# Re-tiling a 32-head attention and an MLP on one Trainium2 core: head quads outermost, scores in row strips, the second product in column strips, a quarter of the exponentials on VectorE, every queue's order planned ahead

## Chip, core and metric

The kernel runs on one core of one Trainium2 chip. The metric is device time in microseconds (us), the median of several runs; lower is better. The engines in what follows are TensorE (PE; its weight loads are PEld), VectorE (DVE), ScalarE (ACT), GpSimd (POOL) and SyncE (SP, which here only issues DMAs). PSUM has eight banks, each 128 partitions by 512 f32; SBUF is the large on-chip memory.

## What is computed

An attention branch `a` and an MLP branch `b` on the same input, mixed by a per-row gate `g`. S = 2048 rows, D = 640, H = 32 heads of Dh = 20, F = 1536; all inputs are bf16.

```python
g = sigmoid((x * gate_w).sum(-1, keepdims=True))
q, k, v = split_heads(x @ wqkv)                    # 32 heads of 20
p = softmax(einsum("bhqd,bhkd->bhqk", q, k) * 20**-0.5)
a = merge_heads(einsum("bhqk,bhkd->bhqd", p, v)) @ wo
h = x @ w1 + b1
b = (h * tanh(softplus(h))) @ w2                   # mish
out = g * a + (1 - g) * b
```

The softmax needs 32 x 2048 x 2048 exponentials: as tiles of 128 keys by 1,024 (two heads by 512 queries) that is 1,024 tiles.

## The kernel before

**Tiling.** The outer loop runs over four chunks of 512 query rows (`qc`); inside it, 16 groups of two heads (`emit_group`, L387); inside that, 16 key tiles `j` of 128 keys. One such step is called a slot here; there are 4 x 16 x 16 = 1,024.

**A slot.** Two matmuls (L395) make scores, keys on the partitions and 512 queries along the row, for two heads; each contracts over only 20 rows and sits in its own 32-row strip of the PE array (`tile_position`). They write `Sp`, two PSUM banks. One ACT instruction (L406) takes exp of the whole 128 x 1024 tile into `E` (bf16, two buffers). Then eight pairs of weight load and matmul (L412) use each 128 x 128 block of `E` as weights and stream the 21 columns of `VA` (20 values and a column of ones, which sums the denominators) into `acc`. After 16 slots DVE takes the reciprocal of the denominators (L421) and scales into `O_qc` (L423).

**Filler work.** Everything else waits in queues of small units, and `pump_slot` (L351) emits units after each slot as long as a credit (460 per slot in the first chunk, 340 later) pays for their cost: K projections (`kt_units`, L143, cast at L150), V projections (`v_units`, L186, cast L193), Q projections (`qt_unit`, L208, cast L215), the MLP's first product and mish (`mlp_ht_unit`: L223, then an exp on ACT at L231, four DVE passes and a DVE reciprocal at L241), its second product (`mlp_b_units`, L261), and for the chunk before, transposes of the attention output (L288) and the output projection (L304, L318) with the gate mix (L311 to L329). What is left at a chunk's end is emitted in one go (`drain_all`, L378).

**Start and end.** x is brought in transposed by one DMA transpose (L88) and, per chunk, a smaller one (L439). The first K and V projections (L143, L171) wait for it. The last chunk's output projection comes after all exponentials. A Tile scheduler keeps the order in which the code emits; each engine runs its own queue in that order and waits on semaphores.

**PSUM.** `Sp` has two buffers of two banks, `acc` two, the filler units two banks in all.

Of the kernel before, what the change touches and what calls it, by code (L numbers as in the profile page):

```python
# [8 lines left out]
P = 128  # L10
ACT = mybir.ActivationFunctionType
ALU = mybir.AluOpType
F32 = mybir.dt.float32
BF16 = mybir.dt.bfloat16


@with_exitstack
def kernel(
# [12 lines left out]
    nc = tc.nc  # L31

    _, S, D = A_x.shape
    F = B_w1.shape[1]
    H = 32
    DH = D // H
    KT = D // P
    FT = F // P
    NS = S // P
    QC = 512  # L40
    NQC = S // QC
    NU = QC // P
    NPAIR = H // 4
    NG = H // 2
    ROWB = 32
    inv_sqrt_dh = float(DH) ** -0.5
    CB = 512
    CH = CB // 2

    x2d = A_x[0]  # L50
    out2d = out[0]

    consts = ctx.enter_context(tc.tile_pool(name="consts", bufs=1))
    wqp = consts.tile([P, KT, NPAIR, P], BF16, tag="wqp")
    ident = consts.tile([P, P], BF16, tag="ident")
    wo_sb = consts.tile([P, KT, D], BF16, tag="wo_sb")
    w1_sb = consts.tile([P, KT, F], BF16, tag="w1_sb")
    w2_sb = consts.tile([P, FT, D], BF16, tag="w2_sb")
    b1bf = consts.tile([P, FT], BF16, tag="b1bf")
    b1f = consts.tile([P, FT], F32, tag="b1f")  # L60
    g_t = consts.tile([P, NS], F32, tag="g_t")
    kT_all = consts.tile([P, NPAIR, S], BF16, tag="kT_all")
    VA = consts.tile([P, NS, H, DH + 1], BF16, tag="VA")

    aps = ctx.enter_context(tc.tile_pool(name="aps", bufs=2, space=bass.MemoryType.PSUM))
    xtc_pool = ctx.enter_context(tc.tile_pool(name="xtc", bufs=2))
    qtc_pool = ctx.enter_context(tc.tile_pool(name="qtc", bufs=3))
    e_pool = ctx.enter_context(tc.tile_pool(name="e_pool", bufs=2))
    opool = ctx.enter_context(tc.tile_pool(name="opool", bufs=1))
    otpool = ctx.enter_context(tc.tile_pool(name="otpool", bufs=1))  # L70
    actpool = ctx.enter_context(tc.tile_pool(name="actpool", bufs=1))
    mishp = ctx.enter_context(tc.tile_pool(name="mishp", bufs=2))
    bpool = ctx.enter_context(tc.tile_pool(name="bpool", bufs=2))
    smallp = ctx.enter_context(tc.tile_pool(name="smallp", bufs=2))
    dpool = ctx.enter_context(tc.tile_pool(name="dpool", bufs=1))
    outp = ctx.enter_context(tc.tile_pool(name="outp", bufs=2))

    xt_ctx = ExitStack()
    xt_ctx.__enter__()
    xtpool = xt_ctx.enter_context(tc.tile_pool(name="xtpool", bufs=1))  # L80
    xT = xtpool.tile([P, KT, S], BF16, tag="xT")

    stage_ctx = ExitStack()
    stage_ctx.__enter__()
    stpool = stage_ctx.enter_context(tc.tile_pool(name="stpool", bufs=1))
    Wq = stpool.tile([P, KT, D], BF16, tag="Wq")
    nc.scalar.dma_start(Wq, A_wqkv[:, 0:D].rearrange("(kt p) c -> p kt c", p=P))
    nc.sync.dma_start_transpose(  # L88
        out=xT[:, :, :], in_=x2d.rearrange("s (kt p) -> s kt p", p=P)
    )  # L90
    wv0 = xtpool.tile([P, KT, 4 * DH], BF16, tag="wvp", bufs=2)
    nc.scalar.dma_start(
        out=wv0[:, :, :],
        in_=A_wqkv[:, 2 * D : 2 * D + 4 * DH].rearrange("(kt p) c -> p kt c", p=P),
    )
    gw = xtpool.tile([P, KT, 1], BF16, tag="gw")
    nc.scalar.dma_start(gw, gate_w.rearrange("(kt p o) -> p kt o", p=P, o=1))
    wk0 = xtpool.tile([P, KT, P], BF16, tag="wkp", bufs=2)
    nc.gpsimd.memset(wk0, 0.0)
    for r in range(4):  # L100
        col0 = 64 * (r // 2) + ROWB * (r % 2)
        nc.scalar.dma_start(
            out=wk0[:, :, col0 : col0 + DH],
            in_=A_wqkv[:, D + r * DH : D + (r + 1) * DH].rearrange(
                "(kt p) c -> p kt c", p=P
            ),
        )
    nc.sync.dma_start(b1bf, B_b1.rearrange("(ft p) -> p ft", p=P))
    nc.gpsimd.dma_start(wo_sb, A_wo.rearrange("(kt p) c -> p kt c", p=P))
    nc.gpsimd.dma_start(w1_sb, B_w1.rearrange("(kt p) c -> p kt c", p=P))  # L110
    nc.gpsimd.dma_start(w2_sb, B_w2.rearrange("(ft p) c -> p ft c", p=P))

    nc.gpsimd.memset(wqp, 0.0)
    for h in range(H):
        p, r = divmod(h, 4)
        col0 = 64 * (r // 2) + ROWB * (r % 2)
        nc.gpsimd.tensor_copy(
            out=wqp[:, :, p, col0 : col0 + DH],
            in_=Wq[:, :, h * DH : (h + 1) * DH],
        )  # L120
    stage_ctx.__exit__(None, None, None)
    make_identity(nc, ident)
    nc.vector.tensor_copy(b1f, b1bf)
    nc.gpsimd.memset(VA, 1.0)

    def kt_units(p, wk=None):
        if wk is None:
            wk = xtpool.tile([P, KT, P], BF16, tag="wkp", bufs=2)
            nc.gpsimd.memset(wk, 0.0)
            for r in range(4):  # L130
                h = 4 * p + r
                col0 = 64 * (r // 2) + ROWB * (r % 2)
                nc.sync.dma_start(
                    out=wk[:, :, col0 : col0 + DH],
                    in_=A_wqkv[:, D + h * DH : D + (h + 1) * DH].rearrange(
                        "(kt p) c -> p kt c", p=P
                    ),
                )

        def chunk(sc):  # L140
            pk = aps.tile([P, CB], F32, tag="t")
            for kt in range(KT):
                nc.tensor.matmul(  # L143
                    pk[:, 0:QC],
                    lhsT=wk[:, kt, 0:P],
                    rhs=xT[:, kt, sc * QC : (sc + 1) * QC],
                    start=(kt == 0),
                    stop=(kt == KT - 1),
                )
            nc.vector.tensor_copy(  # L150
                out=kT_all[:, p, sc * QC : (sc + 1) * QC], in_=pk[:, 0:QC]
            )

        return [(1200, (lambda sc=sc: chunk(sc))) for sc in range(NQC)]

    def v_units(p, wv=None):
        if wv is None:
            wv = xtpool.tile([P, KT, 4 * DH], BF16, tag="wvp", bufs=2)
            nc.sync.dma_start(
                out=wv[:, :, :],  # L160
                in_=A_wqkv[:, 2 * D + 4 * p * DH : 2 * D + 4 * (p + 1) * DH].rearrange(
                    "(kt p) c -> p kt c", p=P
                ),
            )

        def unit(st):
            pv = aps.tile([P, CB], F32, tag="t")
            for kt in range(KT):
                lhsT = xT[:, kt, st * P : (st + 1) * P]
                if p == 0:  # L170
                    nc.tensor.matmul(  # L171
                        pv[:, 0 : 4 * DH],
                        lhsT=lhsT,
                        rhs=wv[:, kt, :],
                        start=(kt == 0),
                        stop=False,
                    )
                    nc.tensor.matmul(
                        pv[:, 4 * DH : 4 * DH + 1],
                        lhsT=lhsT,  # L180
                        rhs=gw[:, kt, 0:1],
                        start=False,
                        stop=(kt == KT - 1),
                    )
                else:
                    nc.tensor.matmul(  # L186
                        pv[:, 0 : 4 * DH],
                        lhsT=lhsT,
                        rhs=wv[:, kt, :],
                        start=(kt == 0),  # L190
                        stop=(kt == KT - 1),
                    )
            nc.vector.tensor_copy(  # L193
                out=VA[:, st, 4 * p : 4 * p + 4, 0:DH],
                in_=pv[:, 0 : 4 * DH].rearrange("p (h d) -> p h d", d=DH),
            )
            if p == 0:
                nc.scalar.activation(
                    g_t[:, st : st + 1], pv[:, 4 * DH : 4 * DH + 1], ACT.Sigmoid
                )  # L200

        return [(260, (lambda st=st: unit(st))) for st in range(NS)]

    def qt_unit(p, xTc, qTc_p):
        def unit():
            pq = aps.tile([P, CB], F32, tag="t")
            for kt in range(KT):
                nc.tensor.matmul(  # L208
                    pq[:, 0:QC],
                    lhsT=wqp[:, kt, p, 0:P],  # L210
                    rhs=xTc[:, kt, 0:QC],
                    start=(kt == 0),
                    stop=(kt == KT - 1),
                )
# [312 lines left out]
```

## Time and profile before

Three runs took 1384.87, 1405.74 and 1419.17 us; the median is 1405.74 us. The profiled execution's span, from the first to the last instruction, is 1383.0 us, so it belongs with the fastest of the three.

| | busy us | share of the span | instructions |
|---|---|---|---|
| PE (matmuls) | 1235.3 | 89% | 12384 |
| PEld (weight loads) | 589.6 | 43% | 12384 |
| ACT | 1053.3 | 76% | 1138 |
| DVE | 463.9 | 34% | 1093 |
| POOL | 28.6 | 2% | 51 |

The profile also gives the TensorE clock that was granted, as a share of full speed: its mean is 0.608. Matmuls are pipelined and their ends are modelled, so a matmul's listed duration holds some latency, and the distance between starts is the better measure of what one costs. The DMA engines moved 16.91 MB, 12 GB/s over the span. The first exponential starts at 64.3 us.

### The profile page before, as it was taken

What the parts mean: (1) busy time and instruction counts of PE and PEld (TensorE: products, weight loads), DVE (VectorE), ACT (ScalarE), POOL (GpSimd) and SP (SyncE); (2) the same over time, 40 slices, a digit from 0 to 9 for tenths busy, and PEclk for the clock granted to TensorE, in tenths of its full rate; (3) what the DMA queues carried; (4) which work ended last, traced back from release to release, by engine and by line L of the source; (5) the groups of instructions that cost most, each with busy time, mean ns of one, the idle gap of its engine ahead of it and who ended that gap; (6) DMA issues with size and microseconds to landing.
All of it is one profiled execution on the core that took longest, in us unless ns stands there. A gap on an engine that the chain in (4) does not pass through costs nothing.

```text
span 1383.0 us, 28359 instructions
## 1 busy us (share of the span) xinstructions
PE 1235.3 (89%) x12384; PEld 589.6 (43%) x12384; DVE 463.9 (34%) x1093; ACT 1053.3 (76%) x1138; POOL 28.6 (2%) x51
## 2 busy tenths in 40 slices
PE   0699999988999988998889998998889988998887
PEld 0354444544444444443434444443434444453333
DVE  0222222377722576410101477410001476510002
ACT  0286666987768877698998777698998787699995
POOL 7000000000000000000000000000000000000000
PEclk9975555975585555795555555695555555695555
DMA  9600000000000000000000000000000000000000
GB/s 185 109 8 7 8 7 7 2 1 1 13 8 11 11 1 1 1 21 1 1 1 11 11 1 1 1 2 1 1 2 6 16 2 1 1 2 1 1 1 20
DMA packets 53086, 16.91 MB, mean 12 GB/s; under 512 B 49408, under 2 KB 52096, under 8 KB 52960
## 3 DMA queue, kind: packets, MB, share of 16 engines
q1 hardware_dynamic: 47456, 9.30, 4.6%
q0 software_dynamic: 912, 4.75, 1.2%
q10 hardware_dynamic: 4592, 1.03, 0.6%
q8 instruction: 97, 1.59, 0.5%
q14 instruction: 29, 0.24, 0.1%
HBM read 7.21 MB, written 2.62 MB: 7 GB/s over the span
## 4 chain that ended last, share of the span: by engine, by line
PE 67%; ACT 25%; issue 3%; DMA 3%; DVE 1%; ACTq 0%
PE Sp L395 26%; ACT E L406 25%; PE acc L412 15%; PE ph L223 8%; PE pk L143 5%; PE pb L261 4%; DMA xT<-in_A_x_dram 3%; PE pq L208 3%; PE pa L304 3%; PE pv L186 3%; PE pt L288 1%; ACTq L406 0%; PE pv L171 0%; ACT e_sb L231 0%; DVE d L311 0%
## 5 line engine op out<-in xcount | busy, mean ns | idle before, releaser
L406 ACT ACTIVATE E<-Sp 128x1024 bf16<-128x1024 f32 x1024 | 1006.0, 1022 | 223.6 <-PE Sp L395 213.0
L395 PE MATMUL Sp<-qTc_p,kT_all 20*128 20x512 bf16 x2048 | 589.2, 559 | 0.0
L412 PEld LDWEIGHTS <-E 128*128 128x128 bf16 x8192 | 335.7, 106 | 471.1 <-ACT E L406 376.9
L412 PE MATMUL acc<-VA,E 128*128 128x21 bf16 x8192 | 398.1, 182 | 95.5 <-ACT E L406 93.5
L241 DVE RECIPROCAL rd<-rd 128x256 f32<-128x256 f32 x96 | 167.4, 1744 | 0.8
L395 PEld LDWEIGHTS <-kT_all 20*128 20x128 bf16 x2048 | 104.3, 98 | 51.5 <-issue 18.2
L223 PE MATMUL ph<-xTc,w_sb 128*128 128x256 bf16 x480 | 119.0, 403 | 0.1
L421 DVE RECIPROCAL rden<-acc 128x8 f32<-128x8 f32 x64 | 12.4, 193 | 297.4 <-PE acc L412 297.4
L223 PEld LDWEIGHTS <-w_sb 128*128 128x128 bf16 x480 | 51.7, 128 | 57.4 <-issue 42.6
L234 DVE SCALAR_TENSOR_TENSOR e_sb<-e_sb 128x256 f32<-128x256 f32 x96 | 40.4, 421 | 100.5 <-ACT e_sb L231 99.6
L215 DVE CAST qTc_p<-pq 128x512 bf16<-128x512 f32 x32 | 22.1, 691 | 148.8 <-PE Sp L395 98.6
L231 ACT ACTIVATE e_sb<-ph,b1f 128x256 f32<-128x256 f32 x96 | 45.4, 473 | 33.8 <-PE ph L223 29.9
L143 PE MATMUL pk<-xT,wk 128*128 128x512 bf16 x140 | 66.0, 548 | 0.0
L208 PE MATMUL pq<-xTc,wqp 128*128 128x512 bf16 x160 | 64.5, 492 | 0.0
L261 PE MATMUL pb<-w_sb,actT 128*128 128x512 bf16 x192 | 58.0, 419 | 0.1
L150 DVE CAST kT_all<-pk 128x512 bf16<-128x512 f32 x32 | 22.1, 691 | 96.3 <-PE pk L143 96.3
L186 PE MATMUL pv<-wv,xT 128*128 128x80 bf16 x560 | 50.7, 237 | 0.0
L193 DVE CAST VA<-pv 128x80 bf16<-128x80 f32 x128 | 30.4, 243 | 57.7 <-PE pv L186 51.5
L143 PE MATMUL pk<-xT,wk_118 128*128 128x512 bf16 x20 | 7.2, 544 | 44.4 <-DMA xT<-in_A_x_dram 44.4
L243 DVE SCALAR_TENSOR_TENSOR actT<-ph,b1f,rd 128x256 bf16<-128x256 f32 x96 | 45.8, 478 | 0.1
L186 PEld LDWEIGHTS <-xT 128*128 128x128 bf16 x560 | 33.4, 117 | 23.2 <-issue 23.0
L261 PEld LDWEIGHTS <-actT 128*128 128x128 bf16 x384 | 28.5, 101 | 33.3 <-issue 24.1
(101 smaller groups left out, 351.9 us busy)
## 6 DMA issues: line engine op xcount, KB each, us to landing
w_sb<-in_B_w_dram POOLq DMA_DIRECT2D x2, 1920.0 KB, 31.1
out_dram<-ot SPq DMA_DIRECT2D x16, 160.0 KB, 1.8
Wq<-in_A_wqkv_dram ACTq DMA_DIRECT2D x1, 800.0 KB, 4.9
wo_sb<-in_A_wo_dram POOLq DMA_DIRECT2D x1, 800.0 KB, 24.5
wv<-in_A_wqkv_dram SPq DMA_DIRECT2D x7, 100.0 KB, 2.3
wk<-in_A_wqkv_dram SPq DMA_DIRECT2D x28, 25.0 KB, 2.6
wv_114<-in_A_wqkv_dram ACTq DMA_DIRECT2D x1, 100.0 KB, 10.7
wk_118<-in_A_wqkv_dram ACTq DMA_DIRECT2D x4, 25.0 KB, 29.7
```

What stands on the lines that cost most here:

```text
L143: nc.tensor.matmul(pk[:, 0:QC], lhsT=wk[:, kt, 0:P], rhs=xT[:, kt, sc * QC : (sc + 1) * QC], start=(kt == 0), stop=(kt == KT - 1),)
L186: nc.tensor.matmul(pv[:, 0 : 4 * DH], lhsT=lhsT, rhs=wv[:, kt, :], start=(kt == 0), stop=(kt == KT - 1),)
L208: nc.tensor.matmul(pq[:, 0:QC], lhsT=wqp[:, kt, p, 0:P], rhs=xTc[:, kt, 0:QC], start=(kt == 0), stop=(kt == KT - 1),)
L223: nc.tensor.matmul(ph[:, 0:CH], lhsT=w1_sb[:, kt, ft * P : (ft + 1) * P], rhs=xTc[:, kt, half * CH : (half + 1) * CH], start=(kt == 0), st ...
L231: nc.scalar.activation(e_sb, ph[:, 0:CH], ACT.Exp, bias=b1f[:, ft : ft + 1], scale=1.0)
L241: nc.vector.reciprocal(out=rd, in_=rd)
L243: nc.vector.scalar_tensor_tensor(out=actT[:, ft, half * CH : (half + 1) * CH], in0=ph[:, 0:CH], scalar=b1f[:, ft : ft + 1], in1=rd, op0=AL ...
L261: nc.tensor.matmul(tile_[:, 0 : col1 - col0], lhsT=actT[:, ft, u * P : (u + 1) * P], rhs=w2_sb[:, ft, col0:col1], start=(ft == 0), stop=(f ...
L304: nc.tensor.matmul(pa[:, :], lhsT=oT[:, ct, u * P : (u + 1) * P], rhs=wo_sb[:, ct, 0:CB], start=(ct == 0), stop=(ct == KT - 1),)
L395: nc.tensor.matmul(Sp[:, QC * t : QC * (t + 1)], lhsT=kT_all[base + ROWB * t : base + ROWB * t + DH, p, j * P : (j + 1) * P,], rhs=qTc_p[b ...
L406: nc.scalar.activation(E[:, :], Sp[:, :], ACT.Exp, scale=inv_sqrt_dh)
L412: nc.tensor.matmul(acc[:, u, t, 0 : DH + 1], lhsT=E[:, QC * t + P * u : QC * t + P * (u + 1)], rhs=VA[:, j, h, 0 : DH + 1], start=first, s ...
```

## The change

The program is written anew; only the arithmetic's outline stays.

- **Loops.** Heads go in quads (four heads), eight of them, outermost; the four query chunks inside; 16 key tiles inside that. K and Q of a quad are kept as `kT`, `qT`, 32 rows per head (20 used, the rest zero), two buffers. Only quad 0 is projected in this layout; the others are projected in blocks of 32 columns, written to DRAM (`kD`, `qD`) and read back strip by strip (`strips_try`), before their quad begins.
- **Scores in row strips.** A pass issues the two matmuls of one tile of 1,024 for ACT (into `SA` or `SB`, two banks each) and, when `SD` is free, two more for DVE, in the four 32-row strips (`try_pass`).
- **Exponentials.** Of the 1,024 tiles ACT takes 742. DVE takes 282: it adds a constant to the scaled score, clips at 0 and writes int16, whose bits read as bf16 are about a power of two (`Z[0]`); two more int16 additions make copies moved by 35 and 83 (`Z[1]`, `Z[2]`), and the second product adds up all three.
- **Second product.** `VA` (32 columns per head: 20 values, ones, zeros) is now the weights, and `E` or `Z` the moving operand with 512 columns; four heads write four 32-partition strips of `acc` (`try_pv`). All projections and the MLP are made in the same four column strips (`mm4`). The result is transposed with respect to before, so the denominators are row 20 of each strip: they go to DRAM, come back as 128 x 16 for a DVE reciprocal, go out again and are read back spread over 32 partitions; POOL multiplies (`group_end`). The normalised output goes to DRAM (`oD`), and is read back at the end for the output projection (`final_loads`, `finish`).
- **MLP.** The hidden layer is kept for 1,024 rows; mish is one table function on ACT, eight instructions of 128 x 3072.
- **Start.** x comes in by plain DMA and is transposed on PE. The gate's sigmoid is made of exp and a DVE reciprocal.
- **Order.** The code first plays the whole program through with constants for durations and latencies, picks what each engine does next (a pass first, then due filler, then second products), and then emits all instructions in that order (`tc.manual_schedule`).
- **PSUM.** `SA`, `SB`, `SD` two banks each, `acc` one, one bank `misc` for all filler (at the start `SD` serves as two more).

| engine queue | rows before | rows after |
|---|---|---|
| PE: matmuls | 12384 | 10728 |
| PE: changes between row strips and anything else | about 2 per slot | 1484 in all |
| ACT: exp tiles 128 x 1024 | 1024 | 742 |
| DVE: exp tiles / int16 additions | 0 / 0 | 282 / 564 |
| DMAs issued by SP | 57 | 508 |

```diff
+QSCALE = UNIT * float(DH) ** -0.5          # UNIT = 128 / ln 2, folded into q
+SHIFTS = (35.0, 83.0)
+ZBIAS = 128.0 * 127 - 251.8
...
+    def mm4(outs_, lhs, rhs, start, stop):
+        for k in range(4):
+            nc.tensor.matmul(
+                outs_[k], lhsT=lhs[k], rhs=rhs[k], start=start, stop=stop,
+                tile_position=(0, 32 * k),
+            )
...
+            nc.tensor.matmul(
+                S_[:, k * QC : (k + 1) * QC],
+                lhsT=kT[32 * t : 32 * t + 32, j * P : (j + 1) * P],
+                rhs=qT[32 * t : 32 * t + 32, g.c * QC : (g.c + 1) * QC],
+                start=True, stop=True, tile_position=(32 * t, 0),
+            )
...
+                op.fn = lambda: nc.scalar.activation(E, Sx, ACT.Exp, bias=0.0, scale=1.0 / UNIT)
...
+                op.fn = lambda: nc.vector.tensor_scalar(
+                    out=Z[0], in0=SD, scalar1=ZBIAS, scalar2=0.0, op0=ALU.add, op1=ALU.max)
...
+                        a = Op("DVE", 0.34, lambda k=k: nc.vector.tensor_scalar(
+                            out=Z[k + 1], in0=Z[0], scalar1=SHIFTS[k], scalar2=None, op0=ALU.add), [op], prio=2)
...
+                    lambda t=t, k=k, e=e, st=st, sp=end_ty: nc.tensor.matmul(
+                        acc[32 * t : 32 * t + 32, :],
+                        lhsT=VAs[(g.q // 2) % 2][:, e["j"], g.q % 2, t, :],
+                        rhs=e["ap"][:, k * QC : (k + 1) * QC],
+                        start=st, stop=sp, tile_position=(0, 32 * t),
+                    )
...
+            d1 = dma(dD[row : row + 4, :], av, [ev], prio=0)
+            d2 = dma(den[n], dD[row : row + 4, :].rearrange("t (a b) -> (t a) b", b=16), [d1], prio=0)
+            rc = new("DVE", 0.2, lambda: nc.vector.reciprocal(den[n], den[n]), [d2], prio=1)
+            d3 = dma(rD[row : row + 4, :].rearrange("t (a b) -> (t a) b", b=16), den[n], [rc], prio=0)
+            d4 = [
+                dma(rb[32 * t : 32 * t + 32, :], rD[row + t : row + t + 1, :].to_broadcast([32, QC]), [d3], prio=0)
+                for t in range(4)
+            ]
+            mu = new("POOL", 1.25, lambda: nc.gpsimd.tensor_tensor(out=o, in0=a, in1=rb, op=ALU.mult), d4, prio=0)
...
+            nc.scalar.activation(v, v, ACT.Mish, bias=0.0, scale=1.0)
...
+    emits.sort(key=lambda e: (e[0], e[1]))
+    with tc.manual_schedule():
+        for _, _, fn in emits:
+            fn()
...
-            E = e_pool.tile([P, 2 * QC], BF16, tag="E")
-            nc.scalar.activation(E[:, :], Sp[:, :], ACT.Exp, scale=inv_sqrt_dh)
-                    nc.tensor.matmul(
-                        acc[:, u, t, 0 : DH + 1],
-                        lhsT=E[:, QC * t + P * u : QC * t + P * (u + 1)],
-                        rhs=VA[:, j, h, 0 : DH + 1],
-                        start=first,
-                        stop=last,
-                    )
```

## The prediction

> **What bounds the kernel now.** First the page's busy times and granted clock, then the chain of waits, then the costliest groups.
>
> ```profile
> PE 1235.3 (89%) x12384; PEld 589.6 (43%) x12384; DVE 463.9 (34%) x1093; ACT 1053.3 (76%) x1138; POOL 28.6 (2%) x51
> ...
> PEclk9975555975585555795555555695555555695555
> ...
> PE 67%; ACT 25%; issue 3%; DMA 3%; DVE 1%; ACTq 0%
> ...
> L406 ACT ACTIVATE E<-Sp 128x1024 bf16<-128x1024 f32 x1024 | 1006.0, 1022 | 223.6 <-PE Sp L395 213.0
> ```
>
> The chain is two thirds PE, and PE stood at half its clock in most slices; ACT lost 213.0 us waiting for scores. So the kernel is a PE kernel at a low clock with an exp kernel close behind. The windows show both states (columns: length, then PE, PEld, DVE, ACT, POOL busy, granted clock, DMA share, GB/s):
>
> ```profile
> 86.00:243.00 157.00, 157.00 (x1414) 71.59 (x1411) 35.13 (x118) 99.00 (x98) 2.52 (x4) 0.50 0.07 7
> 245.00:283.00 38.00, 37.39 (x555) 21.70 (x553) 14.38 (x52) 35.53 (x38) 0.00 (x0) 1.00 0.01 2
> 892.00:927.00 35.00, 34.79 (x434) 18.25 (x431) 5.68 (x18) 33.78 (x36) 0.00 (x0) 1.00 0.01 2
> ```
>
> At half clock PE is full and ACT busy 63% (99.00 of 157). At full clock ACT is busy 93.5% (35.53 of 38) and 96.5% (33.78 of 35). What a slot costs PE stands in the timeline:
>
> ```profile
> 907.40 0.38 PE L261 MATMUL pb<-w_sb,actT 128*128 128x512 bf16 x1
> 907.71 0.39 PE L395 MATMUL Sp<-qTc_p,kT_all 20*128 20x512 bf16 x2
> 908.03 0.36 PE L412 MATMUL acc<-VA,E 128*128 128x21 bf16 x8
> 908.32 0.39 PE L395 MATMUL Sp<-qTc_p,kT_all 20*128 20x512 bf16 x2
> ...
> 1375.14 1.24 PE L304 MATMUL pa<-wo_sb,oT_prev 128*128 128x512 bf16 x5 [0.41 <-DVE d L311]
> ```
>
> At full clock five 512-column matmuls take 1.24 us with 0.38 of latency at the end: 0.215 a piece. One of them ahead of a strip pass is followed after 0.31, so a change into or out of strips costs 0.095. The two strip matmuls together are followed after 0.32: they run side by side. Eight pairs of load and 21-column matmul are followed after 0.29: 0.036 a pair, a floor per pair. At half clock:
>
> ```profile
> 88.11 0.61 PE L143 MATMUL pk<-xT,wk 128*128 128x512 bf16 x1
> 88.52 0.41 PE L412 MATMUL acc<-VA,E 128*128 128x21 bf16 x8
> 88.86 0.61 PE L395 MATMUL Sp<-qTc_p,kT_all 20*128 20x512 bf16 x2
> 89.40 1.03 PE L143 MATMUL pk<-xT,wk 128*128 128x512 bf16 x2
> ```
>
> 512 columns 0.41 to 0.42, a pair of strips with its change 0.54 (so 0.12 a change), a small pair 0.0425 (0.34 for eight).
>
> **ACT after.** Exps run back to back at 0.95 (17 in 16.22 us from 915.20, the last 1.02 long). 742 x 0.95 = 705. Mish, 8 x 3072 elements: no row has it; the exp row gives 3 x 1.022 = 3.07 each, the 256-element exp of L231 (473 ns) and the 1,024-element one give a slope of 0.715 ns and so 2.49; I take 2.8, x8 = 22 (20 to 25). Four table loads at 1.28 past the first = 5, some PSUM copies 2. Gone: 282 exps (268) and L231's 96 (45.4). Sum 734, against 1053.3 busy before.
>
> **PE after, at full clock.** 742 passes x 0.215 = 160 (four strips cost what two cost, by the pair). Second product: 3176 matmuls in fours = 794 quads; filler of 512 columns: 748 quads. Column strips are in no row. Lower end, side by side as the row strips do: 0.215 a quad; upper end, one after another: 0.86. I take 0.215, since the nearest row is a strip row, and keep both: 1542 x 0.215 = 332. 608 quads of 128 or 160 columns x 4 x 0.036 = 88. 1484 changes x 0.1 = 148. 80 transposes, 8. Sum 736: as much as ACT. At half clock: 312 + 1542 x 0.42 (648) + 608 x 0.17 (103) + 1484 x 0.12 (178) + 8 = 1249.
>
> The Trainium skill (TensorE: Matmul & The Clock Gate, Part 3) gives three column strips a speedup of 2.38, four row strips 3.07; an estimate of 3.07 for columns would put a quad at 0.28 and add 100 us to PE. No row here shows it, and the sum does without.
>
> **DVE after.** An exp tile reads 1,024 f32 from PSUM: casts of 512 take 691 ns, of 80 243, so 1.04 ns an element, 1.22 less the 0.08 by which neighbours overlap (four L423 in 0.52, 187 each) = 1.15; x282 = 324. The int16 additions have no row. From SBUF a 256-element f32 scalar op takes 286 where the two-tensor one takes 419: two per cycle by two ports. A 16-bit copy from PSUM takes 424 for 512 where f32 takes 691: two by packing. Both together give 0.34 back to back; only one of them 0.61; neither 1.15. I take 0.34, both halves being shown: x564 = 192 (344, 649). The other PSUM readers, some 200, about 135. Sum 650, under ACT; with 0.61, 805, with 1.15, 1108.
>
> **New waits.** Per group, `reciprocal` of the denominators now waits for two DMA hops. Small DMAs land in 1.8 (L337) to 2.6 us (wk), SP spends 0.33 to 0.56 issuing one. In the new DVE order three to nine instructions worth 4.6 us on average stand between the copy of `acc` and this reciprocal, so it stalls 0 to 1 us, 32 times; behind it wait exp tiles and additions, and for these PE's second products and the next `SD` pass. I take it within ACT's slack: 0, at most 32, no gain possible from a wait that was not there. SP issues 508 DMAs, 170 to 280 us of its queue, not an engine's path; the strip loads of a quad (8 x 0.56 + 2.6 = 7 us) are asked for a quad ahead, some 90 us of cover; without it 7 x 7 = 49. POOL's 32 multiplies (about 1 us each by its rows) are on the path only in the last group.
>
> **Start and tail.** Before, the first exp starts at 64.3 because the DMA transpose lands after 43.6. Now 13 of the 16 x tiles stand ahead of the first pass in PE's order, so it waits for nearly all 2.6 MB: at the first slice's 185 GB/s 14 us, plus landing, 17. After the last exp: copy, four hops of 2.2, POOL, then five output units through one bank (six quads, a change, an eviction of 0.69 each) and the last store: 0.7 + 9 + 1 + 14 + 3 = 28.
>
> **Sum.** PE and ACT are level, as in the two full-clock windows above, so I let ACT be busy 93.5% as in the worse of them: 734 / 0.935 = 785. 17 + 785 + 28 = 830 of span; 2 us lie outside it before (1384.87 against 1383.0). The median stood 1.5% over the profiled run; I add 1%: **840 us**.
>
> **The clock, where a rule meets a row.** After, streaming is 160 + 332 + 37 (the small quads, by columns) of some 785, 67%; in the window from 892 it was about 63% (scores 22, second product 7, filler 34, by the counts of matmuls and their columns). So it should stay up. But between 86 and 243 PE was never idle and stood at 0.50: only runs of about five whole-array 512s (pq, pb) raised it. The new order holds such runs (16 to 28 matmuls of second product or filler in a row), and two long ACT stretches of mish, 11 us each, in which PE may thin out and drop.
>
> The Trainium skill (the same page, "HAM oscillation") says to avoid idle gaps of over about 3 us; by it a PE that never pauses would run at full clock. This trace contradicts that for 157 us, so I follow the row.
>
> **Rivals.**
> - Swings (0.18): the clock drops after mish and where filler is thin, or additions cost 0.61, or hops stall DVE. A quarter of the slots at PE's half-clock rate adds a quarter of 1249 - 736, 128: 900 to 1,040.
> - Half clock throughout (0.10): PE 1249 + 17 + about 14 of tail not PE's = 1,280. For it: the 157 us; against: denser work.
> - Slower: column strips do not run side by side (0.07). Place: the 1,542 quads. At full clock the new kernel costs 436 + 1542 q (17 + 15 + 160 + 88 + 148 + 8 is 436), which meets 1383 at q = 0.61; four matmuls one after another, 0.86, give 1,760. At half clock, 633 + 1542 q, it decides from q = 0.49 on, little above 0.42. For it: four different moving streams at once are not in the trace. Against: rows do it.
> - It does not do what it says: the counts of the new order (742, 282, 10728) say it does; the rest of chance (0.05) is for mixtures.
>
> **Chances and range.** Forecast (full clock, 775 to 900) 0.60. It and the swings hold 8 in 10, so 775 to 1,040; the lower end is 734 + 17 + 24 with ACT never waiting. Faster by over 2% (about what a measurement of this kernel can tell) holds in all cases but the slower one: 0.90; within 2% 0.03, for a half clock with q near 0.49; slower 0.07.
>
> **What would show it.** 742 exps at 0.95 and ACT over 85% busy; granted clock near 1.00 from the first pass on; four column-strip matmuls starting within 0.1 us and the next four 0.215 later; additions of about 0.42 as listed; a first exp near 17 us and a last one 28 before the end. A clock of 0.5 in long stretches, quads 0.3 apart or more, or additions at 0.7 would make it wrong.

## The result and the profile after

Four runs of the changed kernel took 828.65 to 833.94 us, median 829.42; four of the kernel before 1384.87 to 1419.17, median 1411.78. Some executions of the kernel before fall into a slower state, so the ratio is taken over fast runs alone: 0.601, with a 95% interval of 0.597 to 0.606 (the two medians alone would give 0.587): faster. The prediction of 840 was 1.3% high. The profiled execution's span is 828.1 us.

The page of the changed kernel: busy times, granted clock, chain of waits, and the costliest groups (busy, mean ns | idle before).

```profile
PE 761.8 (92%) x10728; PEld 264.3 (32%) x10728; DVE 693.1 (84%) x1141; ACT 727.4 (88%) x767; POOL 58.6 (7%) x50
...
PEclk9999999999999999999999999999869999999999
...
PE 49%; ACT 22%; DVE 21%; issue 6%; DMA 2%; SPq 0%; ACTq 0%; DVEq 0%
...
L985 ACT ACTIVATE E<-SB 128x1024 bf16<-128x1024 f32 x371 | 388.6, 1047 | 26.6 <-PE SD L609 12.9
...
L996 DVE TENSOR_SCALAR Z<-SD 128x1024 int16<-128x1024 f32 x282 | 343.5, 1218 | 29.9 <-PE SD L609 28.4
...
L1006 DVE TENSOR_SCALAR Z<-Z 128x1024 int16<-128x1024 int16 x564 | 230.9, 445 | 8.9
```

The clock, 5 in most slices before, is 9 or more except in two slices near 600 us. ACT lost 213.0 us waiting for scores before; now its two exp groups lose 52.6 (26.6 and 26.0). The chain, two thirds PE before, now goes over all three engines (PE 49%, ACT 22%, DVE 21%). Windows of the changed kernel (length; PE, PEld, DVE, ACT, POOL busy; clock; DMA share; GB/s) show it by stage:

```profile
255.00:270.00 15.00, 10.31 (x138) 4.29 (x138) 6.94 (x13) 14.94 (x8) 0.92 (x1) 0.89 0.15 51
400.00:500.00 100.00, 97.80 (x1250) 29.53 (x1247) 92.56 (x150) 97.49 (x106) 6.64 (x5) 1.00 0.14 39
794.00:828.00 34.00, 19.35 (x454) 10.40 (x448) 11.38 (x22) 0.30 (x1) 1.26 (x1) 1.00 0.18 64
```

In the middle stretch three engines are over 92% busy. The first row is one of the two stretches of mish: ACT is full, DVE half empty, PE thins out and the clock dips. The last is the tail. The timeline of PE (start, duration) shows the price of a pass and of column strips:

```profile
399.64 0.38 PE L609 MATMUL SA<-qT,kT 32*128 32x512 bf16 x1
399.64 0.38 PE L609 MATMUL SD<-qT,kT 32*128 32x512 bf16 x1
399.64 0.39 PE L609 MATMUL SA<-qT,kT 32*128 32x512 bf16 x1
399.65 0.39 PE L609 MATMUL SD<-qT,kT 32*128 32x512 bf16 x1
399.96 0.39 PE L738 MATMUL acc<-Z,VA 128*32 128x512 bf16 x2
...
400.70 0.39 PE L738 MATMUL acc<-Z,VA 128*32 128x512 bf16 x2
400.72 0.29 PE L255 MATMUL misc<-w,hid 128*32 128x128 bf16 x4
400.92 0.38 PE L738 MATMUL acc<-Z,VA 128*32 128x512 bf16 x2
```

Four row strips start within 0.01 us and the next kind of work follows after 0.32, change included. Column-strip work follows column-strip work after 0.22. Even two 512-column matmuls and small ones of another unit, in other strips, start side by side at 400.70 and 400.72.

### The profile page after: what moved, and what is told of

Read it like the earlier page. It is cut to its first block, busy times and chain, and to the rows that moved or that the text cites. A ratio compares the mean times of both kernels' runs of the same rounds, so it can differ in the third digit from the quotient of the medians.

```text
span 828.1 us, 25038 instructions
## 1 busy us (share of the span) xinstructions
PE 761.8 (92%) x10728; PEld 264.3 (32%) x10728; DVE 693.1 (84%) x1141; ACT 727.4 (88%) x767; POOL 58.6 (7%) x50
## 4 chain that ended last, share of the span: by engine, by line
PE 49%; ACT 22%; DVE 21%; issue 6%; DMA 2%; SPq 0%; ACTq 0%; DVEq 0%
ACT E L985 20%; PE misc L255 17%; PE acc L738 15%; DVE Z L996 10%; PE SA L609 8%; PE SB L609 7%; DVE Z L1006 6%; DVE hid L854 2%; DVE nat L401 1%; ACT hid L464 1%; DVE hid L453 1%; DMA hid<-bD 1%; DMA hid<-in_A_x_dram 1%; PE SD L255 1%; DVE accS L765 1%
## 5 line engine op out<-in xcount | busy, mean ns | idle before, releaser
L985 ACT ACTIVATE E<-SB 128x1024 bf16<-128x1024 f32 x371 | 388.6, 1047 | 26.6 <-PE SD L609 12.9
L985 ACT ACTIVATE E<-SA 128x1024 bf16<-128x1024 f32 x371 | 388.9, 1048 | 26.0 <-PE acc L738 20.0
L996 DVE TENSOR_SCALAR Z<-SD 128x1024 int16<-128x1024 f32 x282 | 343.5, 1218 | 29.9 <-PE SD L609 28.4
L738 PE MATMUL acc<-Z,VA 128*32 128x512 bf16 x1692 | 238.1, 385 | 9.1 <-DVE Z L1006 4.6
L1006 DVE TENSOR_SCALAR Z<-Z 128x1024 int16<-128x1024 int16 x564 | 230.9, 445 | 8.9
L738 PE MATMUL acc<-E,VA 128*32 128x512 bf16 x1484 | 213.6, 386 | 0.9 <-DVE VA L332 0.7
L609 PE MATMUL SB<-qT,kT 32*128 32x512 bf16 x742 | 147.9, 384 | 3.9 <-ACT E L985 1.6
L609 PE MATMUL SA<-qT,kT 32*128 32x512 bf16 x742 | 147.0, 384 | 4.5 <-ACT E L985 1.8
L609 PE MATMUL SD<-qT,kT 32*128 32x512 bf16 x564 | 110.7, 384 | 1.9 <-DVE Z L996 1.9
L255 PE MATMUL misc<-w,hid 128*32 128x512 bf16 (+1 forms) x1536 | 87.1, 304 | 3.4 <-DVE nat L401 2.9
```

The lines of the kernel that those rows point to most:

```text
L255: nc.tensor.matmul(outs_[k], lhsT=lhs[k], rhs=rhs[k], start=start, stop=stop, tile_position=(0, 32 * k),)
L609: lambda t=t, k=k: nc.tensor.matmul(S_[:, k * QC : (k + 1) * QC], lhsT=kT[32 * t : 32 * t + 32, j * P : (j + 1) * P], rhs=qT[32 * t : 32 * ...
L738: lambda t=t, k=k, e=e, st=st, sp=end_ty: nc.tensor.matmul(acc[32 * t : 32 * t + 32, :], lhsT=VAs[(g.q // 2) % 2][:, e["j"], g.q % 2, t, : ...
L985: op.fn = lambda: nc.scalar.activation(E, Sx, ACT.Exp, bias=0.0, scale=1.0 / UNIT)
L996: op.fn = lambda: nc.vector.tensor_scalar(out=Z[0], in0=SD, scalar1=ZBIAS, scalar2=0.0, op0=ALU.add, op1=ALU.max)
L1006: a = Op("DVE", 0.34, lambda k=k: nc.vector.tensor_scalar(out=Z[k + 1], in0=Z[0], scalar1=SHIFTS[k], scalar2=None, op0=ALU.add), [op], prio=2)
```

## Experiments

**My theory** after the result: PE at full clock, ACT and DVE are level, so none alone sets the time. **Rival 1**: ACT's exponentials alone do. **Rival 2**: PE alone does. **Rival 3**: the clock is up only because PE is kept dense.

**Is the comparison sound?** The kernels below ran at different times, so the changed kernel was run again, unaltered.

> The changed kernel once more, unaltered. The relieved and the reordered kernels are compared with it across calls, and so maybe across chips; differences of 1 to 2% only mean something if it repeats. If it repeats as its own runs did, 826 to 834 us, then the 7 us of ScalarE's relief, the 15 of VectorE's, the 16 more without most of the MLP's products and the 20 less of the retuned order are real. If the median differs by more than 8 us, the 7 and perhaps the 15 us are not settled.

828.70 us (825.88 to 834.03). It repeats; the differences below are taken from 829.42, and would be 0.7 us smaller (larger where a kernel is slower) from this median.

**One engine relieved at a time, the order kept.** Three edits, each alone and then all together:

```diff
# f_act: ACT
-nc.scalar.activation(E, Sx, ACT.Exp, ...)
+nc.scalar.activation(E[:, 0:896], Sx[:, 0:896], ACT.Exp, ...)
# f_dve: DVE
-out=Z[k + 1], in0=Z[0], scalar1=SHIFTS[k]
+out=Z[k + 1][:, 0:QC], in0=Z[0][:, 0:QC], scalar1=SHIFTS[k]
# f_pe: PE, first layer of the MLP (second: the same with ft)
-mm4(..., kt == 0, kt == KT - 1)
+mm4(..., True, True) if kt == 0 else None
```

> The changed kernel with its order kept instruction by instruction, and only ScalarE relieved: each of the 742 exponentials takes 896 of its 1024 columns (the second product reads the second half of the tile from column 384 on, so 128 columns of the second strip's probabilities are left out). At the 2.751 us that 3072 columns of mish took (0.90 ns a column) 128 columns are 0.11 us, so ScalarE loses about 742 x 0.11 = 82 us of work. My theory, that in the middle of the kernel PE, VectorE and ScalarE are level (97.8, 92.6 and 97.5 of 100 us busy at 400 to 500 us), so that none of them alone sets the time: 805 to 830 us, at most 25 gained. Rival 1, that ScalarE's exponentials alone set it: about 750. Rival 2, that PE alone sets it: 825 to 832.

822.62 us (820.98 to 824.04), 7 less. That is small: its ratio to the kernel before, 0.597 (0.593 to 0.600), is not clear of the 0.599 (0.595 to 0.603) of the run above. One of the two groups of exponentials in this run:

```profile
L985 ACT ACTIVATE E<-SA 128x896 bf16<-128x896 f32 x371 | 340.4, 918 | 47.6 <-PE acc L738 23.4 <-PE SD L609 11.3 <-PE SA L609 10.1
```

Both groups together fell from 777.5 us listed to 680.8, and ACT's busy time, in which overlapping instructions count once, from 727.4 to 681.8. The idle time ahead of the exponentials rose from 52.6 to 90.0, 84 of it ended by PE: most of the busy time that ACT was spared it spent waiting for PE. Rival 1, which asked for 750, falls.

> The changed kernel with its order kept, and only VectorE relieved: each of the 564 shifted additions takes 512 of its 1024 columns (the second product reads that half twice, so half of the two shifted copies is left out). At the shortest addition listed (0.36 us) half the columns spare 0.13 to 0.18 us, 75 to 100 us of VectorE's work in all. My theory (three engines level): 810 to 830 us. Rival 1 (ScalarE alone): 825 to 832. Rival 2 (PE alone): 825 to 832. A time below 780 would say that VectorE alone sets it.

814.49 us (812.11 to 815.25), 15 less. From this run's page, the chain and the additions:

```profile
ACT 44%; PE 38%; issue 8%; DVE 8%; DMA 2%; SPq 0%; DVEq 0%; ACTq 0%
...
L1006 DVE TENSOR_SCALAR Z<-Z 128x512 int16<-128x512 int16 x564 | 151.5, 304 | 8.9
```

The additions fell from 230.9 us listed to 151.5, and DVE's share of the chain from 21% to 8%. Both rivals had expected no change. So DVE, the least busy of the three on the page, was on the path. Where it holds up PE is not shown: PE's listed waits for DVE were short in the changed kernel (1.9 us for `SD`, 4.6 for the additions).

> The changed kernel with its order kept, and only PE relieved: of the MLP's products the first of 5 contraction tiles (first layer) and the first of 12 (second layer) are left in, the others left out. That takes out 192 + 176 column-strip quads of 512 columns (0.22 us each) and 176 of four times 128 columns (about 0.056): 91 us of PE's work, and some of the mode changes with it. My theory (three engines level): 800 to 825 us. Rival 1 (ScalarE alone): 820 to 832. Rival 2 (PE alone): about 740. Rival 3, that PE is granted its full clock only because it is kept this dense: the clock falls to near 0.5 in stretches of hundreds of us, and the time rises to 870 or more although there is less work.

845.53 us (843.57 to 850.54): 16 **more**, with 91 us of PE's work left out. The windows of this run (columns as above):

```profile
240.00:265.00 25.00, 19.40 (x230) 7.18 (x234) 19.15 (x31) 24.90 (x21) 1.27 (x1) 1.00 0.11 33
265.00:270.00 5.00, 2.57 (x36) 0.91 (x32) 1.59 (x3) 4.97 (x5) 0.00 (x0) 0.88 0.22 75
270.00:290.00 20.00, 19.90 (x130) 3.68 (x122) 15.41 (x25) 16.13 (x17) 0.00 (x0) 0.50 0.05 15
290.00:295.00 5.00, 5.00 (x46) 1.31 (x42) 3.92 (x7) 4.50 (x5) 1.27 (x1) 0.73 0.14 43
295.00:355.00 60.00, 53.84 (x585) 18.80 (x582) 56.66 (x94) 59.88 (x66) 2.54 (x2) 1.00 0.12 33
```

After mish, with PE half idle for 5 us, the clock fell to 0.50 for some 20 us. PE was then full at half speed, ACT waited (16.13 of 20), and the clock came back. The later row shows that PE at 90% holds 1.00. The mean clock was 0.935 against 0.985; as a share of each span that is 55 us of clock lost against 12. So rival 3 is right in kind, though not in size: the clock fell in stretches of 3 to 24 us, not of hundreds, and the time rose to 846, not past 870. The trace says what the two did. Of this run's exponentials that directly follow another, 73 start at half clock, 1.41 us after it on average, and 664 at full clock, 0.976 after it; in the changed kernel 735 start at full clock, 0.990 after it, and two at half clock. So, as an estimate, the half clock cost some 30 us (73 x 0.42), and 91 us less of PE's work gave some 9 at full clock (664 x 0.014). By that, PE alone did not set the time either; rival 2 had asked for 740.

> The three reliefs of the runs beside this one together, in the changed kernel's order: exponentials over 896 of 1024 columns, shifted additions over 512 of 1024, and the MLP's products over one contraction tile each (the rest of these is left out). Of about 82 us of ScalarE's work, 75 to 100 of VectorE's and 91 of PE's, all taken out at once, my theory (three engines level) expects 745 to 770 us, much more than the sum of what each relief gives alone. Rival 1 (ScalarE alone): about 750, the same as its own relief alone. Rival 2 (PE alone): about 740, the same as PE's relief alone. Rival 3 (the clock needs a dense PE): 870 or more.

793.58 us (789.71 to 795.4; one run more took 803.06), 36 less. Together they give much more than the sum of the three (7 + 15 - 16 = 6), as level engines should. But I expected 745 to 770, so the theory's size is wrong here. Part of the miss is again the clock (0.961, 31 us lost). The rest is open: ACT, at 85% of the span, stood idle 71.9 us ahead of its exponentials, mostly waiting for PE, and the order planned for the longer durations was kept.

**Undoing VectorE's share.**

```diff
-            if dt is not None and item_ready(ptr[td], now) and abs(ptr[td] - ptr[ta]) < 10:
+            if False:
-        elif dt is not None and min(a_busy_until(t) for t in Atoks) > now + 0.45:
+        elif False:
```

> The change without VectorE's share: all 1,024 exponential tiles go to ScalarE, and none to VectorE; row-strip scores, column-strip second product and an order planned ahead stay (planned anew, since 282 tiles move). The 564 additions and 564 column-strip quads for the shifted copies go with it, so PE loses 564 x 0.22 = 124 us of work and VectorE about 575, and ScalarE gains 282 tiles. By the 0.907 us from one exponential to the next in the changed kernel's trace, ScalarE has 1024 x 0.907 + 29 = 958 us of work; with 18.6 us ahead of the first and 34 behind the last exponential that is 1,010 if it never waits, and 1,060 at the 95% that it is busy in such a stretch. My theory (three engines level, each able to become the bound): 1,010 to 1,070, with ScalarE over 90% busy and PE near 60%. Rival 2 (PE alone sets the time): about 829 - 124 = 705, or 829 if the order holds PE back. Rival 3 (the clock needs a dense PE): the thinner PE falls to 0.5 in long stretches, and its remaining work, twice as long, makes more than 1,100.

1060.19 us (1058.17 to 1062.2), inside what my theory gave, outside the other two. PE is 87% busy on this run's page, not near 60%, and the fall of the clock that rival 3 named did come; its price did not. (The expectation says 564 quads; the count is 282, since 10,728 - 9,600 = 1,128 matmuls are gone, so rival 2's 705 should have read 767.) ACT is now the only bound. Two windows:

```profile
120.00:460.00 340.00, 299.35 (x3992) 99.39 (x3994) 69.37 (x121) 338.08 (x358) 14.01 (x11) 0.99 0.11 31
610.00:930.00 320.00, 286.53 (x1358) 53.57 (x1356) 10.13 (x21) 318.78 (x339) 12.65 (x10) 0.50 0.11 32
```

Once the filler ran out, PE stood at half clock for 320 us and it hardly cost anything: ACT stayed 99.6% busy, with an exponential every 0.944 us (320 / 339), against 0.925 at full clock (173 in the 160 us from 300 on). A low clock matters where PE is the one waited for. VectorE's share is worth 231 us (1060.19 - 829.42).

**Undoing the column packing of the second product.**

```diff
-acc[32 * t : 32 * t + 32, :], ... tile_position=(0, 32 * t)
+acc[32 * sp_ : 32 * sp_ + 32, :], ... tile_position=(0, 32 * sp_)   # sp_: number of the quad in its group, modulo 4
```

> The changed kernel with its order kept, but the four matmuls of each second-product quad are all aimed at one column strip (the strip changes from quad to quad), so that they cannot run beside each other; the sums of the four heads are mixed by that, and the output is left wrong in its attention part. If a matmul of 512 columns takes 0.215 us and the four queue up, a quad takes 0.65 (its last beside the next quad's first) to 0.86 instead of 0.22, and the 794 quads add 340 to 510 us to PE. My theory: PE is then the only bound, 1,150 to 1,340 us, so most of what the change gained rests on the strips. Rival 1 (ScalarE alone sets the time): PE's slack takes part of it, below 1,000. Rival: the strips give nothing because the four never overlapped: 829.

1064.46 us (1059.83 to 1069.09): PE 95% busy, ACT 73%, so PE is the bound as the theory had it, but 235 us are added, not 340 to 510. The busy times and the timeline, which says why:

```profile
PE 1018.7 (95%) x10728; PEld 370.3 (35%) x10728; DVE 704.2 (66%) x1141; ACT 774.6 (73%) x767; POOL 57.9 (5%) x50
...
402.60 0.39 PE L740 MATMUL acc<-E,VA 128*32 128x512 bf16 x1
402.62 0.39 PE L255 MATMUL misc<-w,hid 128*32 128x512 bf16 x2
402.83 0.38 PE L740 MATMUL acc<-E,VA 128*32 128x512 bf16 x1
402.84 0.40 PE L255 MATMUL misc<-w,hid 128*32 128x512 bf16 x3
403.05 0.38 PE L740 MATMUL acc<-Z,VA 128*32 128x512 bf16 x1
403.06 0.38 PE L255 MATMUL misc<-w,hid 128*32 128x512 bf16 x1
403.26 0.38 PE L740 MATMUL acc<-Z,VA 128*32 128x512 bf16 x1
```

The four matmuls of the quad (two with `E`, two with `Z`) stand together in the program's order, ahead of the filler's. They follow one another at 0.215 in their one strip, but six of the filler's, which come after them in the order, start in between, in the other strips. So a strip that is held up holds up only itself, and even this kernel keeps part of the packing: 0.30 is added per quad (235 / 794), not 0.43 to 0.64.

**Column strips where heads do not force them.**

```diff
-mm4([bk[32*k : 32*k+32, :] for k in range(4)], [w1[..., 32*k ...] for k in range(4)], [xT[...]] * 4, ...)
+mm1(bk[:, :], w1[:, kt, ft * P : ft * P + P], xT[...], ...)
```

> The changed kernel, its order kept, with the MLP's and the V projection's products issued as single matmuls with 128 x 128 weights instead of four matmuls in column strips; the same results. It takes out three of four instructions and weight loads of these units and asks what column strips give where heads do not force them. If going between column strips and the whole array costs PE what going into and out of row strips does (0.1 us), and the filler is entered from and left to second products some 300 to 500 times, 30 to 100 us come on top where PE has no slack: 845 to 900 us. If that change is free, PE's work stays as it is or falls a little: 815 to 832. Rival 1 (ScalarE alone sets the time): 825 to 835 in both cases. Rival 3 (the clock needs a dense PE): the whole array streams just as long, so the clock stays as it is.

840.81 us (835.02 to 843.6), 11 more with 2,900 matmuls fewer (7,828); below the first expectation, above the second. In the timeline a whole-array matmul starts 0.33 after a second product (130.85 to 131.18) where strips follow strips after 0.22, so the change costs 0.11 there. That the total stayed below the first expectation fits changes of which only part was on the path; it was not tested. The small gap to the next pass (131.18 to 131.50, 0.32) is what strips pay too.

**Was it only the clock?**

```diff
+            nc.tensor.matmul(Sp[:, 0:QC], lhsT=w1_sb[:, 0, 0:P], rhs=w1_sb[:, 0, 0:QC])   # kernel before, ahead of L395
```

> The kernel before, with one matmul of 128 x 128 weights and 512 columns added ahead of each slot's two score matmuls; it writes the score tile, which the scores then overwrite, so it is pure waste: 1,024 x 0.215 = 220 us of PE's time at full clock, 1,024 x 0.42 = 430 at half. It asks how much of the time before was the granted clock alone. If the clock follows how much PE streams through the whole array, it rises to near 1.00 for most of the span, and a slot takes about what it took in the full-clock stretches (1.0 us) plus 0.1 to 0.215: 1,150 to 1,330 us, faster than before in spite of the waste. If the clock stays near 0.5 (it follows something else): 1,600 to 1,830.

1563.24 us (1556.81 to 1569.67), mean clock 0.717 against 0.608. Neither expectation holds:

```profile
100.00:260.00 160.00, 159.17 (x1932) 77.07 (x1931) 43.43 (x159) 121.11 (x122) 2.52 (x4) 1.00 0.07 7
660.00:820.00 160.00, 160.00 (x1320) 53.75 (x1319) 11.72 (x47) 119.47 (x117) 0.00 (x0) 0.50 0.01 2
```

With the K and V projections as filler the clock now stayed up where it had been 0.50; without them it stood at 0.50 for 160 us although PE never paused and streamed a whole-array matmul in every slot. So neither "never idle" nor "one whole-array matmul per slot" holds the clock. What does is open.

With it stays open how much of the time before was the clock alone. A rough estimate comes from the kernel before itself: in eight stretches at full clock, 235 us in all, an exponential came every 1.13 us (208), in those at half clock, 1,069 us, every 1.30 (824). At 1.13 throughout, 1,024 slots with 64 us ahead and 15 behind make some 1,240 us, 140 less than its span of 1,383. The clock may be worth more than that, since the stretches at full clock also held more filler (12.1 matmuls a us against 8.7).

**Why exponentials follow faster now.**

```diff
-    e_pool = ctx.enter_context(tc.tile_pool(name="e_pool", bufs=2))
+    e_pool = ctx.enter_context(tc.tile_pool(name="e_pool", bufs=4))
```

> The kernel before with four instead of two buffers for the exponentials' output. In the kernel before, back-to-back exponentials started 0.95 us apart, in the changed kernel 0.907, with the same tile and the same function; before, a semaphore instruction stood on ScalarE's queue with every one, since the output buffer and the score tile both had to be waited for. If that second wait is what costs 0.04 us, four buffers do not remove it (the wait is still issued) and the spacing stays 0.95; if it is the buffer coming free late, the spacing falls to 0.91 in the full-clock stretches. Either way PE at half clock sets the time: 1,360 to 1,390 us, no change.

1404.22 us (1398.2 to 1410.25). That is above my 1,360 to 1,390, but the kernel before, run beside it, took 1363.63 to 1419.63, so no change can be read from it. Six exponentials from 245.46 us took 5.76, the last 1.02 of it, so 0.95 apart on average as before: the buffer makes no difference.

The single starts show that the question rests on a mean. In the kernel before they are 915.20, 916.12, 917.08, 918.00 and 919.03: 0.92 apart, and in between 0.96 and 1.03, where the exponential starts 0.1 us after the listed end of its scores (916.98, 918.92). With four buffers they are 0.92 and 0.99 apart in turn. So 0.95 had waits for scores in it; without them it is 0.92 before and 0.905 to 0.92 after. The second wait is not the reason for what is left either: a semaphore instruction stands on ScalarE's queue in the changed kernel too (636 times for 742 exponentials), and there exponentials with and without one just ahead start 0.905 after the one before (the median of each). The cause of the remaining 0.015 is open.

**A better order.** Two kernels:

```diff
# g_best: three banks at the end; x tiles 0 to 3 and their K, Q first; D-only passes during mish
+tail[0] = True ... (once SD is free, Mpool.toks[1:] are given to the output units)
-Unit(-10 + i * 0.01, ...)
+Unit(-10 + 0.2 * (i // 4) + 0.01 * i, ...)
-due = -9.9 + 0.04 * c + ...
+due = -9.9 + 0.2 * c + ...
-elif dt is not None and min(a_busy_until(t) for t in Atoks) > now + 0.45:
+elif dt is not None and act_other[0] > now + 0.3:      # end of the mish instruction on ACT
# g_recal: the same, and
-Op("ACT", 0.946, ...)  Op("DVE", 1.19, ...)  Op("DVE", 0.34, ...)  (0.11, sl)
+Op("ACT", 0.91, ...)   Op("DVE", 1.16, ...)  Op("DVE", 0.37, ...)  (0.06, sl)
```

> The changed kernel with three edits to its order: at the end the output units may use the score tile's two banks too (three banks in all); at the start the first four x tiles, then the first K and Q projection, then the others; and while mish runs on ScalarE, passes for VectorE alone are allowed. Expected: 9 us off the tail (13 output units at a period of 2.33 us through one bank), 5 off the start, and 5 to 10 at the two mish stretches, where VectorE was busy 1.4 of 5 us and the clock fell. If PE is level with the others, a VectorE tile costs PE a pass and three quads, and the mish part gives 0 to 5. In all 805 to 820 us. Rival 1 (ScalarE alone): start and tail count in full, the mish part for 9 tiles more on VectorE: about 805. Rival 2 (PE alone): 815 to 825.

815.69 us (814.04 to 817.69). The first exponential starts at 14.55 instead of 18.61, and 26.4 us follow the last instead of 33.8. Between them 774.9 us passed instead of 775.7: the mish edit filled DVE in the first mish stretch (14.97 of 15 us from 255 to 270, clock 1.00; 13.64 and 0.84 in the second, from 590 to 605) and gave 1 us, as the plan moved only 5 tiles more to DVE (287), and each of these costs PE four matmuls more (10,748 in all). The time fits level engines and PE alone, not ACT alone.

> The kernel with the three edits to the order (output units in three banks, opening reordered, VectorE passes during mish), and four of the durations that its order is planned with set nearer to what the changed kernel's trace shows: an exponential 0.91 instead of 0.946, a group of four small V-projection matmuls 0.06 instead of 0.11, VectorE's exponential tile 1.16 instead of 1.19, its addition 0.37 instead of 0.34. The plan then moves some tiles from VectorE to ScalarE, each of which spares PE two quads (0.44 us). My theory (three engines level): 795 to 813 us. Rival 1 (ScalarE alone sets the time, so more tiles there cost 0.9 each): 815 to 825. Rival 2 (PE alone): 805 to 812.

809.33 us (807.37 to 814.37; ratio to the kernel before 0.592, 0.586 to 0.598), 20 less than the changed kernel, the best of both kernels and all variants that compute the whole result. No slice of its granted clock is below 9 (the trace still has five dips of 3.4 us):

```profile
PE 763.3 (95%) x10716; PEld 265.1 (33%) x10716; DVE 681.9 (84%) x1132; ACT 724.5 (90%) x770; POOL 58.8 (7%) x50
...
PEclk9999999999999999999999999999999999999999
```

Of the 21 us of span, 4 come from the start (first exponential at 14.45), 9.5 from the tail (24.3) and 7.3 from between. ACT takes 745 tiles, DVE 279; each of the three tiles moved spares PE four matmuls (10,716), one quad and not the two that the expectation says. The time lies where level engines (795 to 813) and PE alone (805 to 812) both put it, and not where ACT alone does (815 to 825); it does not choose between the first two. The runs that speak against PE alone are the relieved VectorE and the thinned PE.

## Why the prediction was right, step by step

**The sum** was 17 + 785 + 28 = 830 of span. Measured 18.6 + 775.7 + 33.8 = 828.1: each part was near, and that the errors (+1.6, -9.3, +5.8) nearly cancelled is luck.

**ACT.** 742 exponentials came as counted. Their price of 0.95 was high: 0.907 back to back (400.16 to 403.79 in four steps) and about 0.92 over longer trains, so about 683 instead of 705. The train in the kernel before that gave 0.95 was not back to back: its spacings are 0.92 to 1.03, and the longer ones wait for scores. Mish cost 21.4 us for eight (22 predicted). The share of 93.5% that I took from a stretch of the kernel before came out as 92.8% (714.66 of 770 us, 20 to 790), and 97.5% in the middle.

**PE.** The column strips, the step with the widest bounds (0.215 to 0.86), cost the lower end, 0.22. Passes and changes cost what was priced (0.32 together, 0.11 a change). The small quads were over-sized: 80 of their matmuls, 20 quads, start within 1.12 us (813.33 to 814.45), 0.056 a quad and not 0.144 (with 161 columns 0.068: 60 matmuls in a row from 30.45 us), which takes some 50 us off the term of 88. With it PE's work is about 690, not 736. The floor per pair of load and matmul, 0.036, taken from matmuls that used the whole array, does not hold for strips.

**DVE.** Both halves of the additions' price held: in the trace an exponential tile at 253.95 us is followed after 1.14, a pair of additions at 255.75 after 0.71 (1.15 and twice 0.34 predicted). What I took from it, that DVE lies "under ACT" and so costs nothing, was too simple: relieving it by 79 us gave 15.

**The clock.** It stayed up from the first pass, and the two dips came at mish, as the prediction had it; they cost at most some 12 us of clock. (That only runs of `pq` and `pb` raised the clock before is not quite so: ahead of the rise at 244.6 us stand five `pk`.) The rival "swings" (900 to 1,040) did not come. The thinned kernel shows it was near: with 91 us less of PE's work the same order swings. The streaming shares of 63% and 67% that I compared are no rule: the kernel with a waste matmul in each slot streams some 73% of the time by the same count (120 slots in the 160 us from 660 on) and stands at 0.50. So the clock was forecast rightly on a ground that does not hold, and that is luck.

**New waits.** The reciprocal behind two DMA hops stalled DVE 0.5 us in all, against bounds of 0 to 32. The longest wait of ACT is one that the prediction did not have: after the second mish stretch, from 606.9 to 615.2 us, it stood idle 8.2 of the 52.6 us that its exponentials waited in all. In PE's order 96 filler matmuls stand there between two passes. Most belong to units whose copy DVE makes in four pieces, in 2.84 us, where the order was planned with 1.4; through the one bank `misc` such a unit took 5.27 us (601.61 to 606.88), of which PE, at half clock, waited 2.94 for the copy.

**Start and tail.** The first exponential at 18.6 was near 17, though x's bytes were only part of the reason: 13 x tiles stood ahead of the first pass, as predicted, eight of them ahead of the first projection, and the reordered kernel, with seven and five in these places, gained 4 us with the same bytes. The tail's step that failed is "five output units through one bank": 12 output units were still to come, at a period of 2.33 us (PE 1.47, DVE's eviction and the waits between), and three banks took 7 to 10 us off.

**The rival on the slower side** did not decide: q was 0.22, far from 0.61. The run with one strip per quad puts a price on it: without the packing of the second product alone, and with what overlap that run still had, two fifths of the gain would have gone (235 of 582).

## What to carry to other kernels

When three engines are level, relieving one gives little (here 7 of 82 us on ACT, 15 of 79 on DVE, by estimate 9 of 91 on PE at full clock), and a third more work on one makes it the bound; look instead for long single waits, for the start and the tail. Price strips by the distance between starts in a timeline, and expect work of different units to overlap in different strips. Before thinning a dense PE, look where its gaps will lie: less work can cost time through the clock (16 us here), and a low clock costs next to nothing where PE is not waited for. Before pricing an instruction by a train, look at the single spacings: the mean may hold waits.

## What the runs showed of the hardware

- A clock that had fallen to 0.50 stayed there some 20 us with PE full (270 to 290 in the thinned kernel), 160 us with PE never idle (the kernel with the waste matmul, 660 to 820), and 320 us with PE 90% busy (all exponentials on ACT).
- Column strips are served independently: a matmul that comes later in the program starts, in another strip, ahead of an earlier one that waits for its own (402.62 before 402.83 in the kernel with one strip per quad).
- Exponentials of 128 x 1024 that do not wait start 0.905 to 0.92 us apart, though each is listed with 1.02 and more; two or four output buffers, and a semaphore instruction between them or none, make no difference.
- Four matmuls of 128 columns in column strips take 0.056 us, 512 columns in four strips 0.22; leaving column strips for the whole array costs 0.11.
- An int16 addition of 1,024 elements on VectorE takes 0.36 us, two in 0.71, from SBUF to SBUF.
